# Chunk attention and MoE in one kernel: seven block products for the third tile's mm2, and the fourth tile's AV by rows

## The chip, the cores and the metric

The kernel runs on one core of one Trainium2 chip. The metric is device time in microseconds for one execution, the median of several runs. TensorE (PE) does the matrix products, VectorE (DVE) and ScalarE (ACT) read its banks in PSUM and work on SBUF, GpSimd (POOL) works on SBUF alone, and the queue of SyncE (SP) issues nearly all transfers. Every engine takes its instructions in the order in which the program wrote them.

## The reference

```python
q_c = q.reshape(B, H, nc, chunk, D)             # B=8, H=8, S=576, D=64, chunk=64, nc=9
scores = scale * np.matmul(q_c, k_c.transpose(0, 1, 2, 4, 3))
scores = scores - np.max(scores, axis=-1, keepdims=True)
attn = np.exp(scores)
attn = attn / (np.sum(attn, axis=-1, keepdims=True) + 1e-09)
out = np.matmul(attn, v_c)
# then, with x = out as (4608, 512):
h = x @ w_in                                     # w_in (512, 2048)
g = 0.5 * h * (1.0 + erf(h * inv_sqrt2))
return (g @ w_out).astype(np.float32)            # w_out (2048, 512)
```

Attention stays within chunks of 64 rows. Its output, all heads of a row side by side, goes through two large products with an exact GELU between them.

## The kernel before, in words

The 4608 rows are worked in nine tiles of 512 rows (`t` = 0 to 8): tile t < 8 is the first eight chunks of batch t, tile 8 collects the ninth chunks of all batches. The title's third and fourth tiles are t = 2 and t = 3. Each tile goes through attention (`S`: scores and exponentials, `AV`: the product with V, then the division by the sums, which gives x), through mm1 (x times w_in, and GELU), and through mm2 (GELU's output h times w_out). The attention of tile n = t + 1 is done by small products inside mm2 of tile t, so that TensorE has other products while ACT and DVE work on it.

**Seven products.** A product of 2 by 2 blocks can be done in seven block products in place of eight, if sums of the blocks are formed first. mm1 does so from tile 1 on (`mm1_groups`): four column groups a, b, c, d with the products 1 to 7 each, or three groups and some plain blocks (`p`). mm2 does so from tile `FIRST7` on (`mm2_seven`, banks X, Y, Z and W); before that tile, mm2 is sixteen slots of four 128x512 matmuls (`mm2_slot`). mm2 in seven needs sums of h (`h_sums` by the words h1, h2, h3, then `h_third` and `h_fourth`) and of w_out (`w_sums`, four of them, formed once).

**The order of work.** The order in mm1 is written out by hand as a string of words for each kind of tile (`PROGRAM`, `LATE` for tile 1, `THIRD` for tile 2, `FOUR` from tile 3 on). "3b" is product 3 of group b; "c2a" copies group a's Y bank on ACT ("c3a" on DVE, "c1a" copies X to Y on ACT); "a1b" adds a Z bank on DVE; "g12a" is a GELU on ACT; "p" is a plain block with its GELU; "i0" to "i3" are calls put in at that word. Other work is hung on words (`e1`) or on steps of mm2 (`e2`): in `mm2_seven` on the steps 0 to 5 and, as a pair such as (2, 0), after a half of a product.

**Attention in two forms.** Up to tile 3 (t < `FIRSTX`) AV gives x transposed: `quad_S`, `quad_parts`, `quad_total`, `quad_av`, and `quad_x`, with sums, their exchange between partitions on ACT and transposes of their inverses on DVE. From tile `FIRSTX` on, `rows_av` gives rows: V has a column of ones, so that the sums come out of the same matmuls; `rows_x` divides bank by bank on DVE (five banks of the small pools and the bank that mm2's Z product uses next), and two DMA transposes bring x into the form that mm1 needs. `x_sums` then forms four differences of x blocks on DVE (`T`), which products 4 to 7 of mm1 need.

**Loads.** q, k and v arrive in five rotating stage buffers. GpSimd casts them to bf16 (`pool_cast_q`, `pool_cast_k`, `cast_v_rows`), and DMA transposes on SP's queue bring q and k into place (`flips_of`). Tile 3's k arrives in another order of rows (`ORDERED`), is transposed into a buffer `k_u`, and `in_order` copies it in four parts into place.

**ACT's tables.** `act_table` makes ACT load the table of Exp or Gelu ahead of use.

Of the kernel before, what the change touches and what calls it, by code (L numbers as in the profile page):

```python
# [11 lines left out]
def kernel(  # L12
# [9 lines left out]
    nc = tc.nc  # L22
# [8 lines left out]
    J = 4  # L31
    PC = CH // J
    G = H // 2
# [165 lines left out]
    def in_order(t, g):  # L199

        st = tiles[t]
        if "k_u" not in st:
            st["k_u"], st["kt"] = st["kt"], flips.tile([P, G * J, P], bf16, tag="kt", name="k_t")
        raw = st["k_u"]
        DV(st["kt"][:, g * J:(g + 1) * J].rearrange("p n (e j) -> p (n e) j", j=J),
           raw[:, g * J:(g + 1) * J].rearrange("p j e -> p e j"))

    def cast_v_rows(t, copy, behind=None, parts=(0, 1)):
# [116 lines left out]
                                st["rc", 2 * g2 + c][:].rearrange("p (n u) e -> p n e u", u=2),  # L325
                                op=mybir.AluOpType.mult)

    FIRSTX = 4
    NX = 3

    def by_halves(t):
# [222 lines left out]
        for f in range(n):  # L554
            nc.scalar.activation(st["h"][:, f, :], h_ps[f][:], Act.Gelu)

    FIRST7, FIRST71 = 3, 1

    def h_blocks(t, j0, j1):
        st = tiles[t]  # L560
# [54 lines left out]
    def x_sums(t, which=(1, 3, 2, 4)):  # L615
# [7 lines left out]
        for i in which:  # L623
# [8 lines left out]
              c2c 3a c3b a2a 3b 5c 7c g12a a1b c3c 2c 4b 3c a1c g21a g12b 4c g22b a2b a2c g11c g21c g21b g12c  # L632
              g22c end"""

    THIRD = """begin 1a c1a p 1b c1b 2a 7a 6a c2a 6b 2b 5a g11a c2b g11b 1c c1c c3a a1a p 5b 4a g22a 6c a2a 2c c3b
               g11c 7b a1b i0 3a c2c 3b 7c g21a 5c i1 c3c a1c g12b g12a g22b p 4b g22c p 4c a2b a2c i2 i3 3c g21b
               g12c g21c"""

    FOUR = """begin 1a 1b c1a 1c 6a 7a c1b c2a 6b 5a 2a c1c 6c c2b 5b 7b c3a g11a a1a c3b c2c 3a a1b 1d 4a g22a 4b
               g12a c1d 2b a2a g22b 6d 5c g21a a2b 2d 7c h1 g11b c3c c2d 2c g11d 5d a1c 7d c3d 3c g21b 4c g11c 3b a1d  # L640
               g22c 4d g12c g12b 3d a2c a2d g21c g22d g12d g21d h2 h3"""

    FOURS = range(FIRST7, NT)
    PROGRAMS = {1: LATE, 2: THIRD, **{t: FOUR for t in FOURS}}

    def mm1_groups(t, extra, between={}):
# [83 lines left out]
    def w_sums(which):  # L730

        b11, b12 = w_out_sb[:, :FH, :NH], w_out_sb[:, :FH, NH:]
        b21, b22 = w_out_sb[:, FH:, :NH], w_out_sb[:, FH:, NH:]
        for i in (1, 3):
            if i in which:
                pair = wsum.tile([P, 2, FH, NH], bf16, tag="wsum", name="w_t")
                w_t[i], w_t[i + 1] = pair[:, 0], pair[:, 1]
        of = {1: (b12, b11), 3: (b22, b12), 2: (b22, w_t[1]), 4: (b21, w_t.get(2))}
        for i in which:
            nc.vector.tensor_tensor(w_t[i], *of[i], op=mybir.AluOpType.subtract)  # L740

    def product(out, lhs, rhs, fresh, behind=lambda m: None, ms=range(TH // P)):

        for m in ms:
            for f in range(FH):
                nc.tensor.matmul(out[m], lhs[:, f, m * P:(m + 1) * P], rhs[:, f, :],  # L746
                                 start=fresh and f == 0 and (m == 0 or len(out) == 3), stop=(f == FH - 1),
                                 skip_group_check=True)
            behind(m)
# [8 lines left out]
    def halves(bank):  # L758
        return [bank[:, 0], bank[:, 1]]

    def mm2_seven(t, at={}):
# [24 lines left out]
        h_third(t)  # L786
        product_by_f(halves(Y), h_sum(t, 2), T[2])
        AC(s2[:], Y[:])
        product(halves(X), h[:, 1, :, 0], w[:, 1, :, 0], False)
        AC(y[0][:, :, :NH], X[:])  # L790
        store(t, 0, 0, y)
        product(halves(Y), h_sum(t, 1), T[1], False)
# [172 lines left out]
    with tc.manual_schedule():  # L965
# [126 lines left out]
        for t in range(1, NT):  # L1092
# [4 lines left out]
            if t == 1:  # L1097
                flips_of(2)
                load_v_rows(2, (1,))
                def behind_sums():  # L1100
# [1 line left out]
                    cast_v_rows(2, PO, w_s["c", 4][:, 0, 0, 0:1])  # L1102
                    loads_of_qk(3)
                    pool_cast_qk(3)
                e1 = {"1a": [behind_sums], "p": [lambda: load_v_rows(3)], "end": [lambda: w_sums((1, 3, 2))]}
                e2 = one_tile(2, {5: [lambda: act_table(Act.Gelu)],
                                  8: [lambda: flips_of(3), lambda: loads_of_qk(4)]})
            elif t == 2:
                cast_v_rows(3, PO)
                e1 = {f"i{g}": [lambda g=g: in_order(3, g)] for g in range(G)}  # L1110
                e1["1a"] = [lambda: w_sums((4,))]

                def behind_k():
                    in_order(3, G - 1)
                    nc.gpsimd.tensor_copy(tiles[4]["q"][:, 0, 0, 0, 0:1], tiles[3]["kt"][:, G * J - 1, 0:1])
                    pool_cast_qk(4)
                    flips_of(4)
                    load_v_halves(4)
                    load_qk(5, "q")
                    cast_v_rows(4, PO)  # L1120
                e1[f"i{G - 1}"] = [behind_k]
                e2 = one_tile(3, {8: [lambda: load_qk(5, "k")], 12: [lambda: quad_S(4, (0,))], 13: [lambda: quad_S(4, (1,)), lambda: act_table(Act.Gelu)]})
            elif n < NT:
                def ahead(t=t):
                    if t + 2 < NT:
                        flips_of(t + 2)
                    if t < B - 2:
                        load_v_halves(t + 2, (0,))
                    if t == FIRST7:
                        cast_v_rows(t + 2, PO, parts=(0,))  # L1130
                    if t == B - 1:
                        load_v_halves(B, (1,))
                        cast_v_rows(B, PO)
# [36 lines left out]
                if t + 2 == B:  # L1170
# [3 lines left out]
                        pool_cast_k(B)  # L1174
                        ahead()
                    e1 = {"begin": [lambda: v_behind(last_x, parts=(0, 1))], "g11b": [behind_sums]}
                if t == FIRST7:
                    pool_cast_q(t + 2)
                e2 = {1: [lambda: rows_av(n, tiles[n - 1]["Z"]), lambda: rows_x(n)], 2: [], 3: [], 4: [lambda: x_sums(n)]}
                e2[2] += [next_q, next_k, rest_of_v] if t + 3 < B else [rest_of_v, next_q]  # L1180
                if t + 3 == B:
                    e2[4] += [next_k]
                if n + 1 < NT:
                    e2[1] = [lambda: act_table(Act.Exp)] + e2[1]
                    e2.setdefault(2 if t == FIRST7 else (2, 0), []).extend([lambda: quad_S(n + 1), lambda: act_table(Act.Gelu)])
            phase(t, e1, e2, between=last_rows if t == 1 else {})
# [1 line left out]
_INS = ['q', 'k', 'v', 'moe_w_in', 'moe_w_out']  # L1188
# [26 lines left out]
```

## Time and profile before

| | |
|---|---|
| median of three runs | 269.75 us |
| the runs | 269.55, 271.49, 269.75 us |
| profiled execution | 270.41 us |
| its span | 268.6 us |
| granted TensorE clock, mean | 0.996 |
| TensorE busy | 259.6 us, 97% of the span |
| VectorE busy | 202.1 us, 75% |
| ScalarE busy | 187.1 us, 70% |
| GpSimd busy | 77.0 us, 29% |

The profile is of one execution. Its span is the time from the first to the last instruction, and its own time has some 1.8 us around that. Rows of a timeline give start, length, engine, line, operation, output and input, and in brackets how long the engine had been idle and who ended that. The chain of the work that ended last is a list of pieces with start and length. The DMA engines are busy for most of the first two thirds of the span.

### The profile page before, as it was taken

The page shows a single profiled execution, that of the slowest core. Times are in us where ns is not written, and L with a number is a line of the kernel's source. Part 1 is how long each engine was busy: PE and PEld are TensorE (multiplying, and loading weights), DVE is VectorE, ACT ScalarE, POOL GpSimd, SP SyncE. Part 2 cuts the span into 40 slices and gives each one's busy share as a digit, 9 for nine tenths or more (in the row PEclk, how much of TensorE's full clock was granted, in tenths as well). Part 3 has the DMA queues.
Part 4 walks back from the last instruction along what each step waited for, and adds up shares of the span by engine and source line. Part 5 has one row for each costly group of instructions (what it writes and reads, how often), then busy time and mean ns, then how long its engine had stood idle before and what let it go on. Part 6 is the DMA issues. An engine that isn't in the chain of part 4 may idle for free.

```text
span 268.6 us, 7554 instructions
## 1 busy us (share of the span) xinstructions
PE 259.6 (97%) x3077; PEld 195.6 (73%) x3092; DVE 202.1 (75%) x372; ACT 187.1 (70%) x364; POOL 77.0 (29%) x130
## 2 busy tenths in 40 slices
PE   7989999999999999999999999999999999999993
PEld 3554454476548654888888888888888888888882
DVE  2565775989997879589569956995699769958961
ACT  3466756797767967897689669957995799239700
POOL 3735667361440061441044103500362030000000
PEclk9999999999999999999999999999999999999998
DMA  7999999997979959999899989988886760430005
GB/s 230 285 377 402 395 388 243 237 286 194 336 205 261 244 123 231 279 237 191 232 232 231 177 216 242 264 152 206 237 193 146 166 192 0 89 138 12 2 2 156
DMA packets 127075, 56.59 MB, mean 211 GB/s; under 512 B 103488, under 2 KB 120896, under 8 KB 127040
## 3 DMA queue, kind: packets, MB, share of 16 engines
q1 hardware_dynamic: 126592, 55.59, 79.4%
q10 hardware_dynamic: 448, 0.52, 0.7%
q8 instruction: 24, 0.39, 0.6%
q14 instruction: 11, 0.09, 0.1%
HBM read 36.70 MB, written 9.44 MB: 172 GB/s over the span
## 4 chain that ended last, share of the span: by engine, by line
PE 92%; ACT 2%; DVE 1%; DMA 1%; issue 1%; POOL 0%; SPq 0%; ACTq 0%; DVEq 0%; POOLq 0%
PE y_ps L746 24%; PE h_Y L677 15%; PE y_ps L866 12%; PE h_Z L677 10%; PE h_X L677 10%; PE h_ps L538 6%; PE y_ps L891 4%; PE y_ps L755 4%; PE s_ps L247 2%; PE h_ps L699 1%; DMA arrival<-in_k_dram 1%; PE tp L170 1%; ACT y_ps L782 1%; PE warm L958 1%; PE rc_ps L484 1%
## 5 line engine op out<-in xcount | busy, mean ns | idle before, releaser
L677 PEld LDWEIGHTS <-w_in_s 128*128 128x128 bf16 x480 | 46.8, 98 | 6.1
L677 PEld LDWEIGHTS <-w_in_sb 128*128 128x128 bf16 x360 | 35.1, 98 | 6.5
L677 PE MATMUL h_X<-x,w_in_sb 128*128 128x256 bf16 x240 | 33.7, 272 | 0.0
L677 PE MATMUL h_Y<-x_t,w_in_s 128*128 128x256 bf16 x240 | 32.7, 272 | 0.0
L866 PE MATMUL y_ps<-w_out_sb,h 128*128 128x512 bf16 x137 | 31.7, 379 | 0.9 <-issue 0.8
L746 PEld LDWEIGHTS <-h_s 128*128 128x128 bf16 x304 | 29.7, 98 | 3.6 <-issue 0.2
L746 PEld LDWEIGHTS <-h 128*128 128x128 bf16 x288 | 27.8, 98 | 3.4
L218 POOL CAST v_nat<-arrival 128x1024 bf16<-128x1024 f32 x14 | 14.8, 1061 | 48.4 <-DMA arrival<-in_v_dram 48.3
L164 POOL CAST q_nat<-arrival 128x512 bf16<-128x512 f32 x33 | 19.4, 627 | 28.2 <-DMA arrival<-in_q_dram 19.1
L164 POOL CAST k_nat<-arrival 128x512 bf16<-128x512 f32 x34 | 21.9, 678 | 14.0 <-DMA arrival<-in_k_dram 10.1
L746 PE MATMUL y_ps<-w_t,h_s 128*128 128x256 bf16 x208 | 24.8, 273 | 0.0
L866 PEld LDWEIGHTS <-h 128*128 128x128 bf16 x144 | 13.3, 98 | 15.0 <-issue 0.2
L746 PE MATMUL y_ps<-w_out_sb,h 128*128 128x256 bf16 x192 | 22.9, 273 | 0.0
L963 ACT ACT_TABLE_LOAD x16 | 20.5, 1283 | 1.0 <-PEq L1199 0.7
L684 ACT ACTIVATE h<-h_Y 128x512 bf16<-128x512 f32 x30 | 17.7, 595 | 2.4 <-PE h_Y L677 1.9
L714 ACT COPY h_Y<-h_X 128x512 f32<-128x512 f32 x30 | 17.0, 582 | 2.8 <-PE h_X L677 2.6
L684 ACT ACTIVATE h<-h_X 128x512 bf16<-128x512 f32 x30 | 17.8, 597 | 1.4 <-PE h_X L677 0.6
L677 PE MATMUL h_Z<-x_t,w_in_s 128*128 128x256 bf16 x120 | 18.0, 273 | 0.0
L677 PE MATMUL h_Y<-x,w_in_s 128*128 128x256 bf16 x120 | 17.7, 273 | 0.0
L677 PE MATMUL h_Z<-x_t,w_in_sb 128*128 128x256 bf16 x120 | 17.4, 272 | 0.0
L725 DVE COPY h_a<-h_Y 128x512 f32<-128x512 f32 x8 | 5.5, 692 | 14.1 <-PE h_Y L677 14.1
L254 ACT ACTIVATE pT<-s_ps 128x512 bf16<-128x512 f32 x28 | 14.5, 601 | 2.3 <-PE s_ps L247 2.3
(148 smaller groups left out, 489.4 us busy)
## 6 DMA issues: line engine op xcount, KB each, us to landing
arrival<-in_q_dram SPq DMA_DIRECT2D x7, 1024.0 KB
arrival<-in_k_dram SPq DMA_DIRECT2D x24, 256.0 KB
out_dram<-y_sb SPq DMA_DIRECT2D x23, 256.0 KB
arrival<-in_v_dram SPq DMA_DIRECT2D x20, 256.0 KB
arrival<-in_moe_w_out_dram SPq DMA_DIRECT2D x4, 1024.0 KB
arrival<-in_v_dram SPq DMA_DIRECT2D x30, 128.0 KB
out_dram<-y_sb SPq DMA_DIRECT2D x5, 512.0 KB
arrival<-in_moe_w_in_dram SPq DMA_DIRECT2D x4, 512.0 KB
```

The lines of the kernel that those rows point to most:

```text
L164: copy(st[nm][:, g].rearrange("p j r d -> p r j d"), st[nm + "f"][:, 2 * g:2 * g + 2])
L218: copy(st["v"][:, part[0], part[1], :D], st["vf"][:, part[0], part[1]])
L254: nc.scalar.activation(pT[:].rearrange("p u (c j) -> p u c j", j=J), s_ps[g2][c][:].rearrange("p u (j c) -> p u c j", j=J), Act.Exp, scale ...
L538: nc.tensor.matmul(h_ps[a][:], w_in_sb[:, ks, f * P:(f + 1) * P], st["x"][:, ks, :], start=(ks == 0), stop=(ks == KS - 1))
L677: nc.tensor.matmul(banks[g + name][:, i], lhs[:, kk, i], rhs[:, kk], start=fresh and i == kk == 0, stop=(kk == 1), skip_group_check=True)
L684: nc.scalar.activation(h[:, j:j + 2, m], src[:], Act.Gelu)
L714: AC(banks[g + "Y"][:], banks[g + "X"][:])
L746: nc.tensor.matmul(out[m], lhs[:, f, m * P:(m + 1) * P], rhs[:, f, :], start=fresh and f == 0 and (m == 0 or len(out) == 3), stop=(f == FH ...
L755: nc.tensor.matmul(out[m], lhs[:, f, m * P:(m + 1) * P], rhs[:, f, :], start=False, stop=(f == FH - 1), skip_group_check=True)
L866: nc.tensor.matmul(y_ps[:], st["h"][:, f, ms * P:(ms + 1) * P], w_out_sb[:, f, :], start=(f == 0), stop=(f == FF - 1))
L891: nc.tensor.matmul(tiles[t]["y_ps", ms][:], tiles[t]["h"][:, f, ms * P:(ms + 1) * P], w_out_sb[:, f, :], start=(f == 0), stop=False)
L963: nc.scalar.activation(act_scratch[:], rest[:, 0:1], func)
```

## The change

Tile 2's mm2 goes from sixteen slots to `mm2_seven`; tile 3's AV goes from `quad_av` and its sums to `rows_av` and `rows_x`. Tile 2 keeps three groups and four plain blocks in mm1, in a new order with the words h1 to h3 in it. S and AV of tile 3 and S of tile 4 hang on the steps of `mm2_seven`: S(3) after the X product, AV(3) after the first half of X's second product, S(4) ahead of the last product. The fourth sum of w_out moves from mm1 to just ahead of AV(3). The load of the GELU table moves from the end of tile 2's mm2 to word 5b of tile 3's mm1, and S of tile 5 goes to the middle of the Z product in tile 3's mm2, where the later tiles have it.

Tile 3's V comes in two halves by chunks, the second after the transposes of tile 3's q and k; its cast is in halves too. Tile 3's k is put in order by GpSimd, at the head of its work for tile 2. The loads of tile 5's q and k and of the second half of tile 4's V move to step 2 of tile 2's mm2, and the casts and transposes of tile 4 no longer wait for `in_order`.

```diff
-        DV(st["kt"][:, g * J:(g + 1) * J].rearrange("p n (e j) -> p (n e) j", j=J),
+        PO(st["kt"][:, g * J:(g + 1) * J].rearrange("p n (e j) -> p (n e) j", j=J),
            raw[:, g * J:(g + 1) * J].rearrange("p j e -> p e j"))
...
-    FIRSTX = 4
+    FIRSTX = 3
...
-    FIRST7, FIRST71 = 3, 1
+    FIRST7, FIRST71 = 2, 1
...
-    THIRD = """begin 1a c1a p 1b c1b 2a 7a 6a c2a 6b 2b 5a g11a c2b g11b 1c c1c c3a a1a p 5b 4a g22a 6c a2a 2c c3b
-               g11c 7b a1b i0 3a c2c 3b 7c g21a 5c i1 c3c a1c g12b g12a g22b p 4b g22c p 4c a2b a2c i2 i3 3c g21b
-               g12c g21c"""
+    THIRD = """begin 1a c1a p 1b c1b 2a 7a 6a c2a g11a 5a 6b c2b c3a 1c 2b c1c g11b 5b a1a g22a 4a 6c 7b c2c 3a a2a
+               c3b g21a g12a p a1b 4b 5c g22b 2c a2b 7c g21b g11c 3b c3c 3c a1c 4c g12b a2c h1 g22c g12c g21c p p
+               h2 h3"""
...
-    FOURS = range(FIRST7, NT)
+    FOURS = range(FIRST7 + 1, NT)
...
-        product(halves(X), h[:, 1, :, 0], w[:, 1, :, 0], False)
+        product(halves(X), h[:, 1, :, 0], w[:, 1, :, 0], False, lambda m: also((1, m)))
...
-                e1 = {"1a": [behind_sums], "p": [lambda: load_v_rows(3)], "end": [lambda: w_sums((1, 3, 2))]}
+
+                def first_half():
+                    load_v_halves(3, (0,))
+                    cast_v_rows(3, PO, parts=(0,))
+                e1 = {"1a": [behind_sums], "p": [first_half], "end": [lambda: w_sums((1, 3, 2))]}
                 e2 = one_tile(2, {5: [lambda: act_table(Act.Gelu)],
-                                  8: [lambda: flips_of(3), lambda: loads_of_qk(4)]})
+                                  8: [lambda: flips_of(3), lambda: load_v_halves(3, (1,)), lambda: loads_of_qk(4)]})
             elif t == 2:
-                cast_v_rows(3, PO)
-                e1 = {f"i{g}": [lambda g=g: in_order(3, g)] for g in range(G)}
-                e1["1a"] = [lambda: w_sums((4,))]
-
-                def behind_k():
-                    in_order(3, G - 1)
-                    nc.gpsimd.tensor_copy(tiles[4]["q"][:, 0, 0, 0, 0:1], tiles[3]["kt"][:, G * J - 1, 0:1])
-                    pool_cast_qk(4)
-                    flips_of(4)
-                    load_v_halves(4)
+                for g in range(G):
+                    in_order(3, g)
+                cast_v_rows(3, PO, parts=(1,))
+                pool_cast_qk(4)
+                flips_of(4)
+                load_v_halves(4, (0,))
+                cast_v_rows(4, PO, parts=(0,))
+
+                def loads():
                     load_qk(5, "q")
-                    cast_v_rows(4, PO)
-                e1[f"i{G - 1}"] = [behind_k]
-                e2 = one_tile(3, {8: [lambda: load_qk(5, "k")], 12: [lambda: quad_S(4, (0,))], 13: [lambda: quad_S(4, (1,)), lambda: act_table(Act.Gelu)]})
+                    pool_cast_q(5)
+                    load_qk(5, "k")
+                    load_v_halves(4, (1,))
+                e2 = {1: [lambda: act_table(Act.Exp), lambda: quad_S(3)],
+                      (1, 0): [lambda: w_sums((4,)), lambda: rows_av(3, tiles[2]["Z"]), lambda: rows_x(3)],
+                      2: [loads], 4: [lambda: quad_S(4), lambda: x_sums(3)]}
...
-                    if t == FIRST7:
+                    if t == FIRSTX:
+                        cast_v_rows(t + 1, PO, parts=(1,))
                         cast_v_rows(t + 2, PO, parts=(0,))
...
-                if t == FIRST7:
-                    pool_cast_q(t + 2)
+                if t == FIRSTX:
+                    e1["5b"] = [lambda: act_table(Act.Gelu)]
...
-                    e2.setdefault(2 if t == FIRST7 else (2, 0), []).extend([lambda: quad_S(n + 1), lambda: act_table(Act.Gelu)])
+                    e2.setdefault((2, 0), []).extend([lambda: quad_S(n + 1), lambda: act_table(Act.Gelu)])
```

## The prediction

> **What bounds the kernel now.** I read the engine totals first, then the chain that ended last, then the stages cut at the chain's own changes of line, then each queue (ACT, DVE, SP, POOL) in order of time around the third and the fourth tile (t = 2 and t = 3 in the code).
>
> ```profile
> PE 259.6 (97%) x3077; PEld 195.6 (73%) x3092; DVE 202.1 (75%) x372; ACT 187.1 (70%) x364; POOL 77.0 (29%) x130
> ```
>
> TensorE is busy 97% of the span, so the time falls only where matmuls go, and rises wherever one waits. The stages that the change touches (from, to; length, then busy time of each engine):
>
> ```profile
> 79.53:92.24 12.71, 12.60 (x100) 9.71 (x100) 10.43 (x18) 10.44 (x20) 0.00 (x0) 1.00 1.03 254
> 92.24:108.56 16.32, 15.95 (x255) 7.88 (x257) 13.12 (x27) 12.48 (x30) 5.94 (x11) 1.00 0.78 189
> 108.56:120.94 12.38, 12.38 (x114) 10.93 (x113) 9.07 (x15) 11.09 (x22) 5.82 (x10) 1.00 1.03 260
> 120.94:134.82 13.88, 13.84 (x243) 12.12 (x241) 10.62 (x24) 9.01 (x16) 1.05 (x1) 1.00 0.97 216
> ```
>
> They are mm1 of the third tile, its mm2 (eight products, with S and AV of the fourth tile and S of the fifth inside), mm1 of the fourth, and its mm2 (seven products, with AV of the fifth and S of the sixth). The granted clock is 1.00 in all. The prices on the path come from the chain (start, length, what):
>
> ```profile
> 92.24 1.73 PE y_ps L866 x8
> 93.96 0.67 PE s_ps L247 x64
> ...
> 99.05 0.67 PE av_ps L316 x64
> ...
> 108.56 1.31 PE h_X L677 x12
> ...
> 120.94 1.76 PE y_ps L746 x16
> ...
> 122.78 0.58 ACT y_ps L782
> ...
> 123.41 1.91 PE y_ps L755 x16
> ```
>
> A 512-column matmul takes 1.73/8 = 0.216 us, a block product of sixteen 256-column ones 1.75, a product of mm1 (four of them) 1.31/3 = 0.44, a pass of S or AV 0.67. The row of L782 prices one thing more: a matmul that needs a bank which ACT must first read out starts 123.41 - 122.70 = **0.71 us** after the matmul that filled it.
>
> **The change part by part.** *Matmuls of the third tile's mm2.* Out go 64 at 0.216 = 13.84; in come 7 x 1.75 = 12.25: **-1.6 us**. S and AV keep their 0.67 each, three times. The fourth tile's mm2 shows what such a stage costs beside its matmuls: 13.88 - 12.25 - 2 x 0.67 = 0.3. Without new waits this mm2 would take 12.25 + 2.01 + 0.3 = 14.55 instead of 16.32. But it must hold S *and* AV of one and the same tile, where the fourth tile's held AV of a tile whose exponentials were long done. So I follow the queues from its start, T = 0. These rows give ACT's prices:
>
> ```profile
> 93.54 1.28 ACT L963 ACT_TABLE_LOAD   x1
> 94.83 0.20 ACT L963 ACTIVATE act_scratch<-rest 128x1 f32<-128x1 bf16 x1
> 94.95 2.04 ACT L254 ACTIVATE pT<-s_ps 128x512 bf16<-128x512 f32 x4
> ...
> 107.08 1.28 ACT L963 ACT_TABLE_LOAD   x1
> 108.38 0.20 ACT L963 ACTIVATE act_scratch<-rest 128x1 f32<-128x1 bf16 x1
> 109.09 1.06 ACT L714 COPY h_Y<-h_X 128x512 f32<-128x512 f32 x2 [0.51 <-PE h_X L677]
> ...
> 112.11 0.60 ACT L684 ACTIVATE h<-h_X 128x512 bf16<-128x512 f32 x1
> ...
> 114.49 0.57 ACT L714 COPY h_Y<-h_X 128x512 f32<-128x512 f32 x1
> ...
> 122.78 0.57 ACT L782 COPY y_ps<-y_ps 128x512 f32<-128x512 f32 x1
> 123.37 1.28 ACT L963 ACT_TABLE_LOAD   x1
> ```
>
> From a table load's start to the first exponential it takes 94.95 - 93.54 = 1.41 us, and four exponentials follow at 2.04/4 = 0.51 with 0.60 for the last.
> - X runs 0 to 1.75, S(3) to 2.42; ACT copies X to Y until 2.41, then loads the table: exponentials from 3.82, the last done at 3.82 + 1.53 + 0.60 = 5.95.
> - Y product 2.46 to 4.21, first half of X' to 5.08. Then AV: its first three groups of eight (0.25) run, the fourth writes a bank that the last exponential still reads: 5.33 to 5.95 is a **wait of 0.6**. Behind it on TensorE stands the second half of X'. AV ends at 6.4, X' at 7.3, Y' at 9.05.
> - The dividing of AV's six banks on DVE takes
>
> ```profile
> 123.28 0.19 DVE L362 RECIPROCAL one<-av_ps 128x6 f32<-128x6 f32 x1
> ...
> 126.81 0.42 DVE L363 TENSOR_TENSOR x_r<-y_ps,one 128x256 bf16<-128x256 f32 x1
> 127.15 1.22 DVE L581 TENSOR_TENSOR h_s<-h 128x2048 bf16<-128x2048 bf16 x1
> ```
>
>   127.15 - 123.28 = 3.87 us, the bank lent by Z last. Its first bank (0.69) is done before AV's second part ends, so the last is read at 6.4 + 3.2 = 9.6; Z product is due at 9.05: **wait of 0.55**. The sums of w_out moved in front of the dividing (1.22 at most, as the row of L581 has the same shape) and h_third lie on DVE between about 2 and 4.4, while AV is awaited; without that cover they would go straight to Z. h_fourth is due at 13.8 and done at about 10.9.
> - Z to 11.4, W to 13.15, S(4) to 13.8, last product to **15.55**. Against 16.32 that is **-0.8**, half of what the matmuls give.
>
> *The new order of mm1 in the third tile.* The order has "6a c2a g11a 5a": 5a adds to the bank that c2a must first copy out, and no product stands between (before, 6b and 2b do). That is the hand-over above: **+0.7** on TensorE, with 6b and all else behind it. The in-order copies that left DVE were no bound here; the two plain blocks at the end give ACT and DVE 1.7 us to catch up, so X and the sums h2, h3 come in time.
>
> *The table load moved into mm1 of the fourth tile.* It sat at 107.08, in ACT's idle time before the first copy of mm1 (0.51 idle even after it). That copy stays where it was, 0.53 into the stage: S(4)'s exponentials (2.04 from about 13.5) and the third tile's last copy now fill ACT until then. The load comes at the word 5b, ahead of the first gelu, which came 112.11 - 108.56 = 3.55 into the stage and now comes about 1.3 later (1.41 less 0.1 idle before it). ACT was busy 11.09 of 12.38 there, so the lag dies slowly: the product 1d needs the bank that this gelu reads, 6d the copy that started at 114.49, 4d a later sum. Following the queue I get waits of 0.1, 0.2 and 0.2: **+0.5**; at least 0, at most the whole 1.3.
>
> A page speaks against this step. The Trainium skill, "ScalarE: Activation LUTs", What ACT_TABLE_LOAD costs, puts a switch at about 1283 ns of load and 1380 ns of drain. By it AV's wait and this lag would each grow by 1.25 and the sum would be near +3; the trace has the load (1.28) but the exponential 0.13 behind it, so I go by the row.
>
> *The k order on GpSimd.* Four copies leave DVE (0.60 each) for POOL. No row has such a copy there; the nearest below is a contiguous cast, 0.61, the farthest above what a strided memset costs per element:
>
> ```profile
> L205 DVE COPY k_t<-k_u 128x512 bf16<-128x512 bf16 x4 | 2.2, 600 | 0.0
> ...
> L215 POOL MEMSET v_nat<- 128x32 bf16 x5 | 1.2, 243 | 0.0
> ...
> L1199 POOL MEMSET const-bfloat16-1.0<- 128x1 bf16 x1 | 0.1, 101 | 0.0
> ```
>
> (243 - 101)/31 = 4.6 ns, times 512 = 2.3 us, and so 2.4 to 9.4 for four. I take 1 us each, nearer the cast, which has the same element count.
>
> ```profile
> 78.27 1.05 POOL L218 CAST v_nat<-arrival 128x1024 bf16<-128x1024 f32 x1 [1.55 <-DMA arrival<-in_v_dram]
> 93.68 0.19 POOL L1115 COPY q_nat<-k_t 128x1 bf16<-128x1 bf16 x1 [14.37 <-DMA out_dram<-y_sb]
> 93.94 2.29 POOL L164 CAST q_nat<-arrival 128x512 bf16<-128x512 f32 x4
> 96.17 2.29 POOL L164 CAST k_nat<-arrival 128x512 bf16<-128x512 f32 x4
> ```
>
> POOL was idle 14.37 us there. k's transpose is issued from 80.00 to 82.28 (below); if it lands near 84, the copies end near 88, or 93.4 at the upper price. S(3) is due at 92.95 + 1.75 = 94.7: hidden. Behind them wait the second half of V, then the casts of q4 and k4, then the fifth tile's transposes on SP.
>
> *V in halves, loads moved.* Same bytes in fewer issues (nine become five). SP's rows:
>
> ```profile
> 65.57 10.57 SPq L120 DMA_DIRECT2D arrival<-in_v_dram  x9
> ...
> 80.00 2.28 SPq L197 DMA_TRANSPOSE k_u<-k_nat  x1
> ...
> 82.96 6.99 SPq L102 DMA_DIRECT2D arrival<-in_k_dram  x4
> ...
> 98.48 1.64 SPq L197 DMA_TRANSPOSE k_t<-k_nat  x1
> ...
> 125.32 3.17 SPq L366 DMA_TRANSPOSE x<-x_r  x2
> ```
>
> The second half of V now goes between k_u and the fifth tile's q and k, which come some 2 us later (half a megabyte at the 254 GB/s of that stage). So k4, last issued at 89.95 and there by 96.17, is then cast between 94.2 and 100.6 (2 later, and 2.29 of casts). I take 97.8, near the middle; its transpose is issued by 99.5, and S(4) is due at 92.95 + 13.15 = 106.1: covered. Behind it in SP's order come half of the fifth tile's V (2 issues at 10.57/9 = 1.17), x's two transposes (until 101.8 + 3.17 = 105.0), then q5, k5 (7.0) and the rest of V (3.5): issued by about 116.5 and due, cast, at AV(4), 108.5 + 12.9 + 1.75 = 123.1. Cover: some 5 us after the cast of 1.05; without it AV(4) would wait. DVE sheds the quad work (13.12 busy in the old mm2, 10.62 in the seven-product one), ACT too; neither was the bound there.
>
> *x through DMA transposes.* DVE's last division is at 92.95 + 9.6 = 102.5, x_sums is due about 107.5 and its third sum at 109.8. Before, the same interval was at least
>
> ```profile
> 231.94 0.42 DVE L363 TENSOR_TENSOR x_r<-y_ps,one 128x256 bf16<-128x256 f32 x1
> ...
> 238.74 0.75 DVE L625 TENSOR_TENSOR x_t<-x 128x512 bf16<-128x512 bf16 x2
> ```
>
> 238.74 - 232.36 = 6.4 us, with no wait for x. Mine is 5.0, with 1.1 more before TensorE feels it. The landing itself is not shown: from 1.2 (one issue of the pair 3.17) to 6.4. I take it as hidden.
>
> **Sum:** +0.7 - 0.8 + 0.5 = **+0.45 us**. The profiled execution took 270.41 us for a span of 268.6 and would take 270.9. It lies 0.66 above the median of the runs, 269.75, so for the median I say **270.2 us**.
>
> **The rivals.**
> 1. *All new waits are hidden* (other products slip in, ACT catches up). Then only the matmul term stays: 14.55 against 16.32, -1.8: 268.0 us. For it: TensorE is the bound and every stage after is the same. Against it: the bank of c2a has no other user, and the exponentials cannot start before S.
> 2. *x comes late* (slower). SP keeps order: x's transposes stand behind the fifth tile's k transpose, which waits for POOL's casts, which wait for the four order copies. Place: 6a of the fourth tile, 1.3 after its mm1 begins; it decides once x lands more than 6 us after the last division, near 108.6. At the 2.3 us price POOL is 5 us later than I have it, and x's transposes are issued by 110.0 instead of 105.0; if they land 1.8 after that (half of the 3.6 that the forecast allows), x is there at 111.8, 3.2 past the point, and 0.5 of it covers ACT's lag: +2.7 on the forecast, 272.9 us. For it: the interval is shorter than any that the trace proves. Against it: POOL's and the DMA's idle time in this stretch.
> 3. *ACT's lag is not absorbed* in the fourth tile: 1.3 instead of 0.5: 271.0 us. For it: 11.09 busy of 12.38.
> 4. *The drained table switch* of the page named above: near +3, 272.7 us; two loads in the rows speak against it.
>
> **How the numbers follow.** Forecast 0.50 (own range 269.4 to 270.9), rival 1 0.12, rival 2 0.21, rival 3 0.13, rival 4 0.02, something unseen 0.02. The range takes in 1's nearer side and 2: 268.3 to 273.0. One per cent, 2.7 us, is about what a measurement of this kernel can tell from no change: no case gains that much (the most that can go is 1.8 and the third tile's 0.1), so faster 0.05; rivals 2 and 4 and part of the unseen go to slower, 0.24; the rest is within, 0.71.
>
> **What would show it.** In the profile after: mm1 of the third tile 13.4 long with one gap of 0.7 on TensorE before 5a; its mm2 15.5 with gaps before AV's second part and before Z; a table load about 3.5 us into the fourth tile's mm1 and that stage 12.9. Wrong would be a wait of TensorE on SP's transposes or on POOL at S(3), or an AV that runs through; a third tile shorter by 1.5 us would prove rival 1.

## The result and the profile after

The changed kernel took **273.13 us** (median of ten runs, 271.42 to 275.88), the kernel before 270.0 us in the ten runs beside it (269.55 to 271.49). The ratio is 1.0085 with a 95% interval of 1.0056 to 1.0114: slower by 2.3 us (1.5 to 3.1), and within one per cent. One of the ten runs, 275.88, was in a slower state with a granted clock of 0.992 where the others have 0.995 to 0.998, and the ratio leaves it out; the two medians lie 3.1 us apart. The forecast was 270.2, a loss of 0.45 us. The direction and the class are right; the loss by the ratio is five times as large as forecast. The median lies 0.13 us past the end of the range, 273.0; by the ratio, on the 269.75 that the forecast started from, the time is 272.0 and within it.

The profiled execution took 273.6 us for a span of 271.8. The engine totals of its page:

```profile
PE 259.6 (95%) x3129; PEld 200.5 (74%) x3140; DVE 202.8 (75%) x370; ACT 185.6 (68%) x354; POOL 84.9 (31%) x134
```

TensorE's busy time is the same 259.6 us as before, although the third tile has one block product fewer. A row of matmuls is shown some 0.16 us longer than the distance to the start of the next row (four of mm1: 0.60 for 0.44; sixteen of mm2: 1.91 for 1.75), so up to 0.16 us of each pause counts as busy. So busy time can't say whether the change paid. What it can say is that 3.2 us of span were added with none of it busy. The stages, as windows (from, to; length, then busy time of each engine):

```profile
79.99:93.60 13.61, 12.83 (x99) 9.59 (x99) 9.24 (x17) 10.92 (x21) 6.58 (x8) 1.00 1.00 243
93.60:110.39 16.79, 15.23 (x308) 12.94 (x306) 13.74 (x24) 8.55 (x16) 7.49 (x9) 1.00 1.06 198
110.39:123.44 13.05, 12.64 (x114) 10.93 (x113) 9.66 (x18) 12.65 (x25) 5.69 (x10) 1.00 0.98 261
123.44:137.31 13.87, 13.82 (x242) 12.11 (x241) 10.62 (x24) 9.09 (x16) 1.11 (x2) 1.00 1.20 204
```

The window cuts are a little off from the first matmul of each stage, so I measured every kernel by that matmul on the timeline of PE. All stage lengths below are from there (mm1 and mm2 of the third tile, mm1 and mm2 of the fourth; us):

| kernel | mm1 | mm2 | mm1 | mm2 | sum |
|---|---|---|---|---|---|
| before | 12.70 | 16.33 | 12.38 | 13.88 | 55.29 |
| after | 13.84 | 16.55 | 13.05 | 13.88 | 57.32 |
| order | 13.81 | 16.19 | 13.20 | 13.88 | 57.08 |
| table | 14.20 | 16.65 | 12.40 | 13.87 | 57.12 |
| wsum | 13.93 | 15.79 | 13.05 | 13.88 | 56.65 |
| casts | 13.84 | 15.79 | 13.05 | 13.88 | 56.56 |
| plain | 13.09 | 17.22 | 13.18 | 13.87 | 57.36 |
| three | 13.02 | 16.74 | 12.64 | 13.88 | 56.28 |
| four | 13.02 | 15.17 | 12.63 | 15.84 | 56.66 |
| five | 12.70 | 15.13 | 12.94 | 13.87 | 54.64 |
| six | 12.70 | 19.91 | 12.94 | 13.88 | 59.43 |
| kpool3 | 12.70 | 16.32 | 12.37 | 13.88 | 55.27 |

The four stages lost 2.03 us: +1.14, +0.22, +0.67 and 0. Of the other 1.2 us of span, 0.46 had come before the third tile begins, in the part that the change hardly touches: over the profiles shown here, the first matmul of L866, in the first tile's mm2, comes between 45.48 and 47.01 us, at 46.45 in that of before and at 46.90 in that of after. 0.42 came in the eighth tile's mm1 and 0.3 in pieces before and behind that. Single spans are therefore not compared below; stages are.

Where TensorE waited, by its timeline (start, length, what; in brackets the idle time before and who ended it):

```profile
83.77 1.03 PE L677 MATMUL h_Y<-x_t,w_in_s 128*128 128x256 bf16 x8 [0.73 <-ACT h_a L725]
...
99.75 0.31 PE L347 MATMUL av_ps<-v_nat,pT 64*64 64x65 bf16 x14 [0.20 <-ACT pT L254]
...
104.21 1.91 PE L746 MATMUL y_ps<-w_t,h 128*128 128x256 bf16 x16 [1.31 <-DVE x_r L363]
...
110.22 1.47 PE L677 MATMUL h_X<-x,w_in_sb 128*128 128x256 bf16 x12
...
115.88 0.60 PE L677 MATMUL h_X<-x,w_in_sb 128*128 128x256 bf16 x4 [0.22 <-ACT h L684]
...
117.97 1.03 PE L677 MATMUL h_Y<-x_t,w_in_s 128*128 128x256 bf16 x8 [0.19 <-ACT h_Y L714]
```

In order: 5a behind c2a, AV's second part behind the last exponential, Z behind the dividing, and two small waits in the fourth tile's mm1 behind ACT. Those are the waits that the prediction named, in its places. By starts (the start of the row before, and its 0.44 or 1.75) each is some 0.16 longer than its bracket says: 0.89 for 5a and 1.47 for Z. Z's is far larger than forecast: 1.47 where 0.55 was said. The queue in front of it is DVE's:

```profile
93.26 0.66 DVE L577 TENSOR_TENSOR h_s<-h_s,h 128x512 bf16<-128x512 bf16 x1
93.84 1.09 DVE L576 TENSOR_TENSOR h_s<-h 128x1024 bf16<-128x1024 bf16 x1
94.97 0.98 DVE L577 TENSOR_TENSOR h_s<-h_s,h 128x1024 bf16<-128x1024 bf16 x1
...
96.31 0.87 DVE L577 TENSOR_TENSOR h_s<-h_s,h 128x512 bf16<-128x512 bf16 x1
97.11 1.62 DVE L581 TENSOR_TENSOR h_s<-h 128x2048 bf16<-128x2048 bf16 x1
98.66 1.62 DVE L740 TENSOR_TENSOR w_t<-w_out_sb,w_t 128x2048 bf16<-128x2048 bf16 x1
100.21 0.18 DVE L362 RECIPROCAL one<-av_ps 128x6 f32<-128x6 f32 x1
...
103.73 0.42 DVE L363 TENSOR_TENSOR x_r<-y_ps,one 128x256 bf16<-128x256 f32 x1
```

and beside it GpSimd's (four rows of k4's cast in one):

```profile
84.40 4.18 POOL L205 COPY k_t<-k_u 128x512 bf16<-128x512 bf16 x4 [6.08 <-DMA k_u<-k_nat]
...
92.25 3.15 POOL L164 CAST q_nat<-arrival 128x512 bf16<-128x512 f32 x4 [2.17 <-DMA arrival<-in_q_dram]
96.30 4.46 POOL L164 CAST k_nat<-arrival 128x512 bf16<-128x512 f32 x4 [0.90 <-DMA arrival<-in_k_dram]
```

DVE has no idle time from 92.75, when the sums of h begin, to the end of the dividing: the sums for mm2 run into the dividing. The first reciprocal starts at 100.21, 6.5 us into mm2. The sums of 2048 columns take 1.62 instead of the 1.22 of the row of L581 before, and GpSimd's four casts of k4 take 4.46 instead of 2.29. The sums of h in front of them are long too: where nothing runs on GpSimd, a sum of 128x512 takes 0.42 and one of 128x1024 0.69.

### The profile page after: what moved, and what is told of

Same layout as the page of the kernel before. It is cut to its first block, busy times and chain, and to the rows that moved or that the text cites. A ratio compares the mean times of both kernels' runs of the same rounds, so it can differ in the third digit from the quotient of the medians.

```text
span 271.8 us, 7644 instructions
## 1 busy us (share of the span) xinstructions
PE 259.6 (95%) x3129; PEld 200.5 (74%) x3140; DVE 202.8 (75%) x370; ACT 185.6 (68%) x354; POOL 84.9 (31%) x134
## 4 chain that ended last, share of the span: by engine, by line
PE 56%; DVE 4%; ACT 3%; issue 1%; ACTq 0%
PE y_ps L746 26%; PE h_Y L677 11%; PE h_Z L677 7%; PE h_X L677 7%; PE y_ps L755 4%; PE s_ps L247 1%; DVE x_r L363 1%; ACT y_ps L782 1%; DVE h_s L577 1%; DVE w_t L740 1%; DVE h_s L581 1%; DVE h_s L576 1%; ACT h L684 0%; ACT h_Y L714 0%; DVE h_d L728 0%
## 5 line engine op out<-in xcount | busy, mean ns | idle before, releaser
L746 PEld LDWEIGHTS <-h_s 128*128 128x128 bf16 x352 | 34.4, 98 | 4.1 <-issue 0.2
L746 PEld LDWEIGHTS <-h 128*128 128x128 bf16 x336 | 32.5, 98 | 5.6 <-issue 1.5
L164 POOL CAST q_nat<-arrival 128x512 bf16<-128x512 f32 x33 | 20.3, 653 | 32.2 <-DMA arrival<-in_q_dram 24.9
L164 POOL CAST k_nat<-arrival 128x512 bf16<-128x512 f32 x34 | 24.3, 748 | 15.3 <-DMA arrival<-in_k_dram 11.6
L746 PE MATMUL y_ps<-w_t,h_s 128*128 128x256 bf16 x240 | 28.6, 273 | 0.0
L746 PE MATMUL y_ps<-w_out_sb,h 128*128 128x256 bf16 x224 | 26.9, 273 | 0.0
L866 PE MATMUL y_ps<-w_out_sb,h 128*128 128x512 bf16 x76 | 17.6, 379 | 0.5 <-issue 0.5
L363 DVE TENSOR_TENSOR x_r<-av_ps,one 128x384 bf16<-128x384 f32 (+1 forms) x30 | 15.9, 531 | 1.1
```

The costliest lines, as they stand in the source:

```text
L164: copy(st[nm][:, g].rearrange("p j r d -> p r j d"), st[nm + "f"][:, 2 * g:2 * g + 2])
L363: nc.vector.tensor_tensor(rows[:, s, b0:b0 + nb].rearrange("p b r d -> p (b r) d"), av[:, :, :D], one[:, :2 * nb].to_broadcast([P, 2 * nb, ...
L866: nc.tensor.matmul(y_ps[:], st["h"][:, f, ms * P:(ms + 1) * P], w_out_sb[:, f, :], start=(f == 0), stop=(f == FF - 1))
```

## The experiments

All kernels but `kpool` were timed beside the kernel before; ratios are to that one, 95% in brackets.

### Where the three losses come from

**order**: 6b and 2b go between c2a and 5a, as they stood before.

```diff
-    THIRD = """... 7a 6a c2a g11a 5a 6b c2b c3a 1c 2b c1c g11b 5b a1a g22a 4a ...
+    THIRD = """... 7a 6a c2a 6b 2b g11a 5a c2b c3a 1c c1c g11b 5b a1a g22a 4a ...
```

> The changed kernel with one thing moved: 6b and 2b stand between 6a and 5a in the third tile's mm1, as before the change. Theory (hand-over): the wait of 0.73 us of TensorE ahead of 5a goes, and mm1 of the third tile shrinks from 13.84 us to about 12.9; the whole kernel gains about 0.8 us. Rival (ACT or DVE is the bound of this stage anyhow, the wait only shows where): the wait reappears at a later word of mm1 or at the sums h2, h3, the stage stays above 13.5 and the kernel gains under 0.3.

Measured: 1.0095 [1.0063, 1.0127]; mm1 13.81 against 13.84. The wait at 5a is gone, and one stands at 4a instead:

```profile
84.69 0.60 PE L677 MATMUL h_Z<-x_t,w_in_sb 128*128 128x256 bf16 x4 [0.60 <-DVE h_a L728]
```

My theory of a hand-over at 5a alone falls. Before the change a plain block stood behind a1a (DVE's add of the Z bank that 4a is to fill); in the changed order only 5b stands there, so 4a is next in line to wait. My reading is that mm1 lacks filler, and that taking it from one gap opens the next; plain, below, bears on it.

**table**: S(4) and the GELU table load at step 3 of the third tile's mm2, no load at 5b.

```diff
-                      2: [loads], 4: [lambda: quad_S(4), lambda: x_sums(3)]}
+                      2: [loads], 3: [lambda: quad_S(4), lambda: act_table(Act.Gelu)], 4: [lambda: x_sums(3)]}
...
-                if t == FIRSTX:
-                    e1["5b"] = [lambda: act_table(Act.Gelu)]
```

> The changed kernel with S of the fifth tile and the load of the GELU table both ahead of the W product in the third tile's mm2 (step 3), and no load at word 5b. Theory (table load on a full ACT): mm1 of the fourth tile shrinks from 13.05 us to 12.4 to 12.5 and the kernel gains about 0.6 us. Rival (the fourth tile's mm1 waits for x, which landed at 110.05 us): the stage stays near 13.0 and the gain is under 0.2 us.

Measured: 1.0079 [1.0046, 1.0113]; the fourth tile's mm1 is 12.40 long against 13.05, by its first matmul and that of the next stage:

```profile
110.79 1.47 PE L677 MATMUL h_X<-x,w_in_sb 128*128 128x256 bf16 x12
...
123.19 1.04 PE L746 MATMUL y_ps<-w_out_sb,h 128*128 128x256 bf16 x8
```

The stage is back at what it took before (12.38), so the load at 5b, with S(4) where it stood, costs 0.65; S moved with the load, and the two were not parted. The interval of the whole kernel is too wide to show that much by itself, and this profile's third mm1 was longer (14.20, with a wait of 0.21 for x's sums that after does not have; two of these sums took 1.71 there beside GpSimd's cast of V, against 0.88 for such a pair with nothing beside it).

**wsum**: the fourth sum of w_out is formed at word 1a of mm1 again.

```diff
+                e1 = {"1a": [lambda: w_sums((4,))]}
...
-                      (1, 0): [lambda: w_sums((4,)), lambda: rows_av(3, tiles[2]["Z"]), lambda: rows_x(3)],
+                      (1, 0): [lambda: rows_av(3, tiles[2]["Z"]), lambda: rows_x(3)],
```

> The changed kernel with the fourth sum of w_out formed in the third tile's mm1 (word 1a), as before the change. Theory (DVE comes late to AV's banks): dividing starts some 0.7 us earlier, when AV's second bank is full, Z's wait falls from 1.47 us to about 0.8, and the kernel gains about 0.7 us. Rival (AV's end alone sets the dividing): Z's wait stays within 0.2 us and nothing is gained.

**casts**: GpSimd casts the fifth tile's q and k from the fourth tile's arrivals, which have long landed, so that the casts run earlier. The fifth tile's scores are then those of the fourth tile's q and k; its own are left out.

```diff
+                for nm in "qk":
+                    for g in range(G):
+                        PO(tiles[4][nm][:, g].rearrange("p j r d -> p r j d"), tiles[3][nm + "f"][:, 2 * g:2 * g + 2])
                 cast_v_rows(3, PO, parts=(1,))
-                pool_cast_qk(4)
```

> The changed kernel, but the casts of the fifth tile's q and k read the arrivals of the fourth tile's q and k, which are there earlier (the fifth tile's scores are those of the fourth). So GpSimd casts at about 88.5 to 93 us and is idle while DVE forms the sums of the third tile's mm2; the loads stay. Theory (DVE and GpSimd slow each other on SBUF): h_third and the sum of w_out take 1.22 us again in place of 1.62, the last h sum 0.42 in place of 0.87, the dividing starts 0.8 us earlier and Z's wait falls to about 0.7. Rival (the transfers that arrive then slow DVE): these sums stay at about 1.6 us, and Z's wait stays.

Measured: wsum 1.0087 [1.0059, 1.0116] and casts 1.0071 [1.0035, 1.0106]; mm2 is 15.79 in both, against 16.55, and Z's wait 0.55 in both (0.71 by starts, for 1.47), as expected. Of wsum and then of casts, on PE:

```profile
102.28 1.91 PE L746 MATMUL y_ps<-w_t,h 128*128 128x256 bf16 x16 [0.55 <-DVE x_r L363]
```

```profile
102.24 1.91 PE L746 MATMUL y_ps<-w_t,h 128*128 128x256 bf16 x16 [0.55 <-DVE x_r L363]
```

In casts the same sums stay in the same order in front of the dividing. Its GpSimd and its DVE:

```profile
87.32 2.27 POOL L1117 CAST q_nat<-arrival 128x512 bf16<-128x512 f32 x4
89.55 2.28 POOL L1117 CAST k_nat<-arrival 128x512 bf16<-128x512 f32 x4
91.78 1.04 POOL L218 CAST v_nat<-arrival 128x1024 bf16<-128x1024 f32 x1
```

```profile
91.55 1.55 DVE L576 TENSOR_TENSOR h_s<-h 128x512 bf16<-128x512 bf16 x1
...
95.31 0.42 DVE L577 TENSOR_TENSOR h_s<-h_s,h 128x512 bf16<-128x512 bf16 x1
95.65 1.22 DVE L581 TENSOR_TENSOR h_s<-h 128x2048 bf16<-128x2048 bf16 x1
96.79 1.22 DVE L740 TENSOR_TENSOR w_t<-w_out_sb,w_t 128x2048 bf16<-128x2048 bf16 x1
98.22 0.20 DVE L362 RECIPROCAL one<-av_ps 128x6 f32<-128x6 f32 x1 [0.22 <-PE av_ps L347]
```

The casts of q and k no longer run beside the sums: each of the last three has its old price (0.42, 1.22, 1.22 for 0.87, 1.62, 1.62) and DVE stands ready 0.22 before AV's bank is filled. V's cast now runs beside the first sum of h, which takes 1.55 for 0.42. The rival is out: beside the last two sums the transfers moved 202 GB/s in casts, and 133 in after. The other traces say the same. Over all thirteen kernels, the 185 sums of 128x2048 with nothing of GpSimd beside them took 1.21 to 1.23 us, and the thirteen beside casts of q or k 1.62 to 1.66; of thirty beside a cast of V, 23 kept 1.22 and seven took 1.71 or 2.06. This shows the mechanism: GpSimd's casts and DVE's sums, both in SBUF, slow each other. What decides which of the two gives way is not shown. The Trainium skill, "GPSIMD Engine Reference", 8. Key points, says that GpSimd shares its SBUF interfaces with VectorE, with contention against instructions of two SBUF inputs. The rows agree and add the size (1.62 for 1.22).

### Can the change be mended?

**plain**: order, and one of the two plain blocks at the end of mm1 put back between a1a and 5b.

```diff
-    THIRD = """... g11b 5b a1a g22a 4a 6c ... g22c g12c g21c p p
+    THIRD = """... g11b a1a p 5b g22a 4a 6c ... g22c g12c g21c p
```

> The changed kernel with the third tile's mm1 in this order: 6b and 2b between 6a and 5a, and one of the two plain blocks from the end put back between a1a and 5b (before the change one stood there). Theory (moving 5a alone failed because the next hand-over, from a1a to 4a, had lost its filler too: a plain block of 0.87 us): no wait of TensorE above 0.3 us is left, and the stage shrinks from 13.84 us to 12.7 to 12.9. Rival (DVE and ACT together are too slow for three groups at this pace): the wait turns up again further on and the stage stays above 13.4.

Measured: 1.0099 [1.0073, 1.0125]. mm1 falls to 13.09, 0.75 below after and a little above the 12.7 to 12.9 expected, and mm2 rises to 17.22:

```profile
96.02 1.48 PE L755 MATMUL y_ps<-w_t,h_s 128*128 128x256 bf16 x12 [0.22 <-DVE h_s L577]
...
103.79 1.91 PE L746 MATMUL y_ps<-w_t,h 128*128 128x256 bf16 x16 [1.98 <-DVE x_r L363]
```

The block at the end was time in which DVE caught up with the sums for mm2. Without it the dividing starts 7.2 us into mm2 in place of 6.5, and Z gives the gain back.

**three**: plain, wsum and table together.

> Three edits at once: the order with the plain block put back, the fourth sum of w_out in mm1 (word 1a), S of the fifth tile and the table load at step 3. Theory: the gains add, since they lie in three stages one after the other: mm1 12.7 to 12.9, mm2 15.7 to 15.9, the fourth tile's mm1 12.4; together 40.9 to 41.2 us against 41.41 of the kernel before the change and 43.44 of the changed one, so the whole is at the kernel before or up to 0.4 us better. Rival (x through DMA transposes lands too late for a shorter stage): a wait of TensorE of 0.5 us or more appears at 6a of the fourth tile's mm1, and the three stages stay above 41.5.

Measured: 1.0017 [0.9997, 1.0038]; 42.40 for the first three stages. That is 1.04 less than after, but 1.2 to 1.5 more than I expected. The sums of h still run beside the casts of q4 and k4 (0.88 for 0.42, 1.63 for 1.22), and DVE is late at three places of mm2:

```profile
95.73 1.05 PE L755 MATMUL y_ps<-w_t,h_s 128*128 128x256 bf16 x8 [0.40 <-DVE h_s L577]
...
96.98 0.61 PE L755 MATMUL y_ps<-w_t,h_s 128*128 128x256 bf16 x4 [0.20 <-DVE h_s L577]
...
102.84 1.91 PE L746 MATMUL y_ps<-w_t,h 128*128 128x256 bf16 x16 [0.98 <-DVE x_r L363]
```

The rival has a part as well: the three stages stay above 41.5, and 6a of the fourth tile waits for x, by 0.23 and not by the 0.5 that it named.

**four**: three, with the banks divided in the order 3, 4, 5, 0, 1, 2, so that Z's, number 5, comes third and not last, and the first half of the fifth tile's V loaded behind x's transposes.

```diff
-        for bank in range(6):
+        for bank in (3, 4, 5, 0, 1, 2) if t == FIRSTX else range(6):
...
-                load_v_halves(4, (0,))
-                cast_v_rows(4, PO, parts=(0,))
...
                 def loads():
+                    load_v_halves(4, (0,))
+                    cast_v_rows(4, PO, parts=(0,))
```

> The three edits, and AV's banks of the fourth tile divided in the order 3, 4, 5, 0, 1, 2, so that the bank lent by Z is free after three of six, with the load of the first half of the fifth tile's V moved behind x's transposes on SP. Theory (dividing alone holds Z): Z's wait of about 0.55 us goes and mm2 falls to 15.2 us. Rival (x then binds): mm2 falls all the same, but the fourth tile's mm1 waits for x at 1a or 6a by about what mm2 gained.

Measured: 1.0037 [0.9994, 1.008]. mm2 of the third tile is 15.17 and has no wait of note, as expected. But the V put back in SP's queue is missing a tile later, and the fourth tile's mm2 goes from 13.88 to 15.84:

```profile
123.86 0.57 PE L347 MATMUL av_ps<-v_nat,pT 64*64 64x65 bf16 x48 [1.87 <-POOL v_nat L218]
```

**five**: the old order of mm1 with h1 to h3 in it, the w_out sum and the table load as in three, four's edits, and each cast in time: q4 loaded and cast ahead of the fourth tile's second half of V, the fifth tile's V cast ahead of the sixth's k.

```diff
+    THIRD = """begin 1a c1a p 1b c1b 2a 7a 6a c2a 6b 2b 5a g11a c2b g11b 1c c1c c3a a1a p 5b 4a g22a 6c a2a 2c c3b
+               g11c 7b a1b 3a c2c 3b 7c g21a 5c c3c a1c g12b g12a g22b p 4b g22c p 4c a2b a2c h1 3c g21b
+               g12c g21c h2 h3"""
...
+                                  8: [lambda: flips_of(3), lambda: load_qk(4, "q"), lambda: load_v_halves(3, (1,)), lambda: load_qk(4, "k")]})
...
+                pool_cast_q(4)
                 cast_v_rows(3, PO, parts=(1,))
+                pool_cast_k(4)
...
                     load_v_halves(4, (1,))
+                    cast_v_rows(4, PO, parts=(1,))
+                    load_qk(5, "k")
```

> The edits of the run before, with three repairs: the third tile's mm1 in the order of the kernel before the change (h1 to h3 added), the fifth tile's q loaded and cast ahead of the second half of the fourth tile's V, and the second half of the fifth tile's V loaded and cast ahead of the sixth tile's k. Theory (what was left were queue waits, each behind a transfer or a cast that stands too late): mm1 12.7, mm2 15.0 to 15.3, the fourth tile's mm1 12.4 to 12.6 and its mm2 13.9 again; together about 54.2 us against 55.29 before the change, so the kernel is 0.3 to 0.5% faster than before the change. Rival (each repair only moves the wait): the four stages stay above 55.2 us and the kernel is no faster than before the change.

Measured: 0.9995 [0.9961, 1.0028], 270.46 us beside 270.51. Its first two stages take 27.83 us against 29.03 before, so the change with these edits does pay 1.2 us there. With q4's cast moved ahead, the six sums of h2 and h3 have their lone prices (0.41 to 0.69), and only h_third still takes 1.63. The four stages take 54.64, where I expected 54.2: two waits behind them are in stages that take 0.56 and 0.59 longer (mm1 of the fourth tile 12.94, of the fifth 12.98, for 12.38 and 12.39), and that gives it back:

```profile
118.31 0.60 PE L677 MATMUL h_Z<-x_t,w_in_sb 128*128 128x256 bf16 x4 [0.45 <-DVE h_d L728]
...
134.96 0.61 PE L677 MATMUL h_Y<-x_t,w_in_s 128*128 128x256 bf16 x4 [0.43 <-DVE x_t L625]
```

**six**: five, with all of the fifth tile's V ahead of its q and k transposes on SP.

```diff
+                load_v_halves(4)
                 flips_of(4)
+                cast_v_rows(4, PO)
...
-                    load_v_halves(4, (0,))
-                    cast_v_rows(4, PO, parts=(0,))
...
-                    load_v_halves(4, (1,))
-                    cast_v_rows(4, PO, parts=(1,))
```

> The run before (labelled five) with the whole of the fifth tile's V loaded ahead of that tile's transposes on SP, where the transfers had 4 us of idle time, so that q and k of the sixth tile follow x's transposes at once. Theory (what five gave back were the waits of 0.45 and 0.43 us after late casts and transposes): mm1 12.7, mm2 15.1, the fourth tile's mm1 12.4 to 12.6, its mm2 13.9, and no wait at the fifth tile's 6a: 54.1 to 54.3 us in place of 54.64 (five) and 55.29 (before the change), and the whole is 0.3 to 0.5% faster than before the change. Rival (the transfers' bandwidth binds in this stretch, whatever their order): a wait for x or for V appears in the fourth or fifth tile, and the ratio stays within 0.2% of 1.

Measured: 1.0241 [1.0185, 1.0296], the largest loss. My theory falls: mm1 of the fourth tile stays at 12.94, that of the fifth goes from 12.98 to 12.57 only, and mm2 of the third tile takes 19.91. On SP the V loads stand 5.53 us in front of the transposes, and TensorE waits for the k that comes behind them:

```profile
92.64 5.53 SPq L144 DMA_DIRECT2D arrival<-in_v_dram  x5
98.28 2.20 SPq L197 DMA_TRANSPOSE q_t<-q_nat  x1
100.58 2.90 SPq L197 DMA_TRANSPOSE k_t<-k_nat  x1
```

```profile
105.62 1.05 PE L247 MATMUL s_ps<-q_t,k_t 64*64 64x64 bf16 x64 [3.25 <-DMA k_t<-k_nat]
```

Behind that wait the granted clock is at half for 3.4 us (0.54 while S runs, 0.58 while the W product does): W takes 2.96 us for 1.75 and S 0.98 for 0.67, which adds 1.5 us. Behind the shorter waits of the other runs, up to 1.98 us, it stays at 1.00.

### One part alone

**kpool** and **kpool3** are the kernel before with nothing but the k order on GpSimd (the first hunk of the diff); kpool is a single execution, kpool3 the same kernel timed.

> The kernel before with one part of the change alone: the four order copies of k go to GpSimd. Theory: each takes about 1.04 us there as in the changed kernel (0.60 on DVE), nothing waits for them, and the stages of the third tile stay within 0.1 us of 12.70 and 16.33. Rival (the copies on GpSimd cost time on the path): S of the fourth tile waits for them by 1 us or more, since here they stand at the words i0 to i3, late in mm1.

> The kernel before with the four order copies of k on GpSimd alone, now timed. Theory: nothing on the path changes, so the ratio to the kernel before is 1.000 with both ends of the interval within 0.3%. Rival (DVE freed of 2.4 us in mm1 shortens the sums on the path): faster by 0.3% or more.

Measured: kpool 269.68 us, its GpSimd row

```profile
85.57 4.17 POOL L205 COPY k_t<-k_u 128x512 bf16<-128x512 bf16 x4 [5.30 <-DMA k_u<-k_nat]
```

and kpool3 0.998 [0.9953, 1.0007], with the stages of before to 0.01. This part is neutral alone as far as the interval tells: its lower end lies outside the 0.3% that I expected, and a gain is not proven.

No kernel here beats the one before by more than its interval.

## Why the prediction was right or wrong

**Right: the class, the sign and the places.** The loss of mm1, the two new waits of mm2 and the lag of ACT all appear where the steps put them. By mm2's first matmul, AV's last group ends near 6.4 as the step has it, Y' ends near 9.05, and W, S(4) and the last product run without waits. The sign of the whole is partly luck, since the sign of the mm2 term is wrong and the other two terms outweigh it. No transfer decides, so rival 2 is out for this kernel; so is rival 1, since the waits are there. AV's wait shows as 0.20 where 0.6 was said: the products ahead of it were 0.2 later than in my queue and the rest of the time is spread among them; its end is the forecast's.

**mm1: +0.7 said, +1.14 measured.** The hand-over is real and shows as 0.73 idle. It costs about 0.9, since groups of four that follow each other start 0.44 apart but are shown 0.60 long, so that a gap looks 0.16 too short. Two stretches of about 0.16, ahead of 4b and 4c, whose banks DVE's adds give back, come on top. Of the step, the sentence that the plain blocks at the end give DVE and ACT time held as far as TensorE goes (plain shows what it costs to take one away). On the rest of the order the step put nothing, and that did not hold: order shows that 4a would wait where 5a did.

**mm2: -0.8 said, +0.22 measured. This is the step that failed**, and in it the sentence that the sums "lie on DVE between about 2 and 4.4, while AV is awaited". They ended at about 100.2, 6.5 after the stage's start. The order of the queue was right and its prices were not. The sums of h2 and h3 in front were to be done at about 2; they were done at 97.1, 3.4 after the start, since four of them (0.66, 1.09, 0.98, 0.87) took 3.6 us where they take 2.2 alone. The two sums that I priced by the old row then took 0.4 more each. That is 2.2 us in all, and it is what the casts of q4 and k4 beside them cost. The remark that DVE sheds the quad work and is no bound there fell with it: DVE is busy 13.74 us in that stage, 13.12 before. The rows that bore this were in the trace of before: the casts of q4 and k4 ran between 93.94 and 98.46, and I moved them on in time in the step on V without asking what of DVE runs beside them. Even the price was there, at other tiles: a sum of w_out at 2.06 beside V's cast, where the next one takes 1.21, and a sum of h at 0.83 for 0.42 beside casts of k.

```profile
65.72 1.22 POOL L218 CAST v_nat<-arrival 128x1024 bf16<-128x1024 f32 x1 [6.71 <-DMA arrival<-in_v_dram]
65.95 2.06 DVE L740 TENSOR_TENSOR w_t<-w_out_sb 128x2048 bf16<-128x2048 bf16 x1
...
199.85 3.39 POOL L164 CAST k_nat<-arrival 128x512 bf16<-128x512 f32 x4 [1.56 <-DMA arrival<-in_k_dram]
201.94 0.83 DVE L576 TENSOR_TENSOR h_s<-h 128x512 bf16<-128x512 bf16 x1
```

Either remedy alone, the sum taken away (wsum) or the casts taken away (casts), gives back 0.76 of the 1.00 by which 16.55 exceeds the forecast 15.55: in both the dividing then starts with AV's bank, 5.8 us into the stage, about where the step had it. Z's wait is then 0.71 by starts, where the step forecast 0.55; that is 0.16 of the 0.24 that is left, and I did not settle the rest.

**Table load: +0.5 said, +0.67 measured.** Waits of 0.1, 0.2 and 0.2 were forecast at 1d, 6d and 4d; the trace has 0.22 at 1d and 0.19 at 6d, by starts 0.38 and 0.35, and nothing of note at 4d. ACT's rows:

```profile
113.84 1.28 ACT L963 ACT_TABLE_LOAD   x1
115.14 0.20 ACT L963 ACTIVATE act_scratch<-rest 128x1 f32<-128x1 bf16 x1
115.25 0.58 ACT L684 ACTIVATE h<-h_X 128x512 bf16<-128x512 f32 x1
```

The first gelu comes 5.0 into the stage, 1.41 behind the load's start and 0.13 behind its end, so rival 4 is out. The Trainium skill, "ScalarE: Activation LUTs", What ACT_TABLE_LOAD costs, adds a drain of about 1380 ns to the load; these rows do not have it. By table the whole step, S(4)'s place included, costs 0.65, so rival 3 (1.3) is out too.

**k order on GpSimd: right.** 1.04 us a copy against 1 taken, and hidden, by kpool3 even alone.

**x through DMA transposes: right, but with little margin.** SP issued them from 103.65 to 108.07, and DVE's x sums waited for the landing:

```profile
103.65 4.42 SPq L366 DMA_TRANSPOSE x<-x_r  x2
```

```profile
110.05 0.76 DVE L625 TENSOR_TENSOR x_t<-x 128x512 bf16<-128x512 bf16 x2 [0.80 <-DMA x<-x_r]
```

The last division ended at 104.15, and the landing ended DVE's wait at 110.05, so the pair took 5.9 us to land, where I had 5.0 between the division and the sums and 1.1 more of cover behind it. It was hidden because Z, and all behind it, starts right behind the last division too: from there to 6a it is 7.4 us, as in the forecast (7.3). Where the first of the x sums came 6.4 to 6.5 us behind the last division (order, plain, three), 6a started 0.11 to 0.23 late. V was covered as said: 1.87 of wait appear only in four, which moves it behind x.

**The sum.** +1.14 + 0.22 + 0.67 = +2.03 where +0.45 was said; the timed runs have +2.3 (1.5 to 3.1). What the stages don't show, 0.42 in the eighth tile's mm1 among it, differs from profile to profile (in kernels with the same order there it is 0 to 0.5), and I did not trace it.

## What to carry to other kernels

A saved product pays only if the engines that prepare the next products have the time for it: here one block product less (1.6 us) left DVE's sums, the dividing and the banks to be caught up in less time, and each filler moved from one gap opened another. Price an operation moved on one engine at the hours of the other engine too: look in the trace of before for what runs beside its new place, and take a row's duration from a place where the same things run beside it. Where a sum must be hidden behind a wait, write out its engine's queue from the end of the stage before, with these prices for the rows in front of it too.

## What the runs showed of the hardware

GpSimd's casts from float32 to bf16 and DVE's bf16 additions in SBUF slow each other: beside casts of q or k, 128x2048 on DVE takes 1.62 for 1.22 us, 128x512 up to 0.88 for 0.42 and four 128x512 casts on GpSimd 4.46 for 2.29; beside a cast of V, a 128x512 sum took 1.55 in casts and a 128x2048 sum 2.06 in the kernel before. Not every sum beside a cast is slowed. With the casts taken out of the way the old prices are back. A strided copy in bf16 of 512 columns on GpSimd takes 1.04 us. A pair of DMA transposes of x landed 5.9 us after its last input was written, 2.0 us after SP had issued it (5.4 to 6.5 us after the last input in the six other runs in which DVE waited for it). After TensorE had waited 3.25 us, in six, the granted clock was 0.54 to 0.58 for the next 3.4 us; behind waits of 1.31 to 1.98 us it was 1.00.
